# Three products summed by transfer, another order of casts, conversions and memory in a tuned attention and two-network kernel

## The chip, the cores and the metric

One core of one Trainium2 chip runs the whole program. The metric is the device time of one execution in microseconds; for the kernel before it is 1594.09 us, the median of three runs (1589.73 to 1597.51).

## The reference

```python
def _attn_ref(q, k, v, g_norm):                     # 8 batches, 8 heads, 576 tokens, head 64
    kv = np.einsum('bhsd,bhse->bhde', k, v)
    out = np.einsum('bhsd,bhde->bhse', q, kv)
    rms = np.sqrt(np.mean(out * out, axis=-1, keepdims=True) + 1e-06)
    return (out / rms * g_norm).astype(np.float32)
...
# x: [4608 tokens, 512]; each network has w_in [512, 2048] and w_out [2048, 512]
def _moe_ref(x, w_in, w_out):
    r = np.maximum(x @ w_in, 0.0)
    return (r * r @ w_out).astype(np.float32)
...
def _moe2_ref(x, w_in, w_out):
    h = x @ w_in
    return ((h * np.cos(h)) @ w_out).astype(np.float32)
```

The result is `_moe2_ref(_moe_ref(attention))`. Everything is in float32; the weights arrive as 64-bit floats.

## The kernel before

A matrix value is split into two parts, `h` (rounded by a cast on ScalarE) and `l` (the rest, subtracted on VectorE), and each product is three matmuls: h by h, h by l and l by h. The work has two stages.

Stage one (`run_chunks`, until about 500 us) computes attention and, for the first half of the first network's 2048 inner columns, both matrix products directly. Its sums leave PSUM in `evict` (L397) through the tile `ev` and are stored in the DRAM tensors `p_d`. Between its matmuls it converts the 64-bit weights (`conv_steps`, L165).

Stage two is the slot loop (`run_slots`, L825). A slot is (m, t, q): network m, token tile t, and a group q of 512 inner columns. The first network has two groups left per tile, the second four, and there are five tiles: 10 and 20 slots, k = 0 to 29. Three tiles are twice 512 tokens wide, two are twice 384 (`TILES`). In a slot each of the two matrix products is done as seven products of half-size blocks, numbered 0 to 6 and taken in the order 0, 1, 3, 2, 5, 4, 6. The first matrix product makes h from x blocks (`x_block`, L455: differences of four quarter blocks, cast and rest) and weights `wi`; the second makes output sums from blocks of y (`s_block`, L586: the differences t1, t2 and two more, then cast `gh` and rest `gl`) and weights `ws`. Between them stands the activation: relu and square, or five steps for h·cos(h) (`cos_1` to `cos_5`). The second product of slot k runs 1.25 slots after the first (`LAG2`), so TensorE alternates between the first product of one slot and the second product of an earlier one.

PSUM holds two pairs of banks, FA and FB for first products, SA and SB for second ones. Products 0, 3, 5, 6 add up in one pair, 1, 2, 4 in the other, so each product in a pair must be read before the next one adds to it. In nearly all slots product 1 starts from a copy of product 0, made by ScalarE from one bank to the other (`seed` for F, L650 for S); `HOLD` delays product 1 by a quarter of its length for that copy.

`drain_product` (L646) reads a finished second product and adds it to one of four sums in SBUF; `SUM_OF` names the sum: product 1 goes to (0,0), 2 and 5 to (1,1), 3 and 4 to (0,1), 6 to (1,0). In the first group of a tile in the second network ScalarE writes the first of them as a plain copy. Otherwise either VectorE adds from PSUM (L662), or, for the products in `BY_DMA` and not in the last slot, ScalarE copies PSUM to a tile `part` (L659, pool `t` with two buffers) and GpSimd issues a transfer that adds `part` to the sum:

```python
if m and i in BY_DMA and k < len(slots) - 1:
    part = blocks_of(t, temp([P, 2, 512], F32, "part"))
    nc.scalar.copy(out=part, in_=ps)
    nc.gpsimd.dma_start(out=e, in_=part, accum_op=ALU.add)
else:
    nc.vector.tensor_tensor(out=e, in0=ps, in1=e, op=ALU.add)
```

The order is written as a list of jobs, each with a place in slots (`at`, `pos`, L680); PH is the seventh of a slot that one product takes. The framework then orders each engine's instructions ahead of time and every engine runs its list in order, waiting where an input is not there or a buffer is not free. Seven conversions of the second network's weights run in the slot loop (`late_stream`, L730), each in steps (`Stream.place`, L697).

Memory: stage two's pools `c` (18 tiles: x, h, y, t and g blocks) and `t` (`part` and the temporaries of conversions) and the late conversions' raw tile lie where stage one's pools were (L880-882, opened from the right end of SBUF), so their first use waits until stage one has finished with what lies there.

Of the kernel before, what the change touches and what calls it, by code (L numbers as in the profile page):

```python
# [8 lines left out]
F32 = mybir.dt.float32  # L9
# [13 lines left out]
def kernel(  # L23
# [15 lines left out]
    nc = tc.nc  # L39
# [384 lines left out]
    ORDER = (0, 1, 3, 2, 5, 4, 6)  # L424
    W_OF = (0, 1, 3, 4, 6, 5, 2)
    BLOCKS = {(0, 0): 2, (1, 1): 5, (0, 1): 6, (1, 0): 7}
    S_ORDER = (0, 1, 3, 2, 5, 4, 6)
    BY_DMA = (4, 5, 1, 6)
    SEEDED = 2

    def seeded(k):
# [3 lines left out]
        return seeded(k) and k < len(slots) - 1  # L435

    HOLD = 9
    xb, wi, ws, kept, hs, ys, sums, quads = {}, {}, {}, {}, {}, {}, {}, {}

    def big(pool, dtype, name, ht):  # L440
# [81 lines left out]
    def t_tile(k, dtype, name):  # L522
        return big("c", dtype, name, TILES[slots[k][1]][1])
# [55 lines left out]
    def load_sum(k, d, j):  # L579
# [3 lines left out]
        for b, s0, done, size in pieces(t0 + j * ht, ht, TOK):  # L583
            nc.sync.dma_start(out=e[:, :, done:done + size], in_=p_d[b][:, 2 * d:2 * d + 2, s0:s0 + size])

    def s_block(k, i):  # L586
        m, t, q = slots[k]
        b11, b12, b21, b22 = (ys.get((k, b)) for b in ((0, 0), (0, 1), (1, 0), (1, 1)))

        def minus(out, x, y):  # L590
            nc.vector.tensor_tensor(out=out, in0=x, in1=y, op=ALU.subtract)
            return out

        if i == 3:
            ys[k, "t1"] = minus(t_tile(k, F32, "t"), b12, b11)
            ys[k, "t2"] = minus(t_tile(k, F32, "t"), b22, ys[k, "t1"])
        src = {
            0: lambda: b11,
            1: lambda: b21,
            2: lambda: ys[k, "t1"],  # L600
            3: lambda: ys[k, "t2"],
            4: lambda: b22,
            5: lambda: minus(b12, b22, b12),
            6: lambda: minus(b21, b21, ys[k, "t2"]),
        }[i]()
        gs[k, i] = h, l = [t_tile(k, F32R, f"g{n}") for n in "hl"]
        nc.scalar.copy(out=h, in_=src)  # L607
        nc.vector.tensor_tensor(out=l, in0=src, in1=as32(h), op=ALU.subtract)  # L608
# [77 lines left out]
    class Stream:  # L686
# [9 lines left out]

        def place(self, positions, after, skip=()):  # L697
            for k, (n, item) in enumerate(zip(positions, self.items)):
                steps = (0, 0.07, 0.15, 0.22, 0.3, 0.4, 0.62)
                if n < nA0:  # L700
                    steps = (0, 0.25, 0.5, 0.75, 1.0, 1.25, 1.4)
                if self.use != conv_w or item[0] == "one":
                    at(n, self.use, *item)
                    steps = (after,)
                for d in steps[:-1]:
                    at(n + d, conv_part, *item)
                if k not in skip:
                    at(n + steps[-1], self.advance)
# [20 lines left out]
    w_stream.place(w_at, 0.5, range(2 * NH - NRAW, 2 * NH - NRAW + 2))  # L729
    late_stream = Stream(load_w, conv_w, [("pairs", 1, p, 0) for p in range(1, 2 * NP)])  # L730
    at(pos(0.15), late_stream.advance)
    late_stream.place([pos(0.45 + 1.05 * k) for k in range(5)] + [pos(9.9), pos(10.85)], 0)

    kv_stream = Stream(load_kv, kv_mm, [(b, c) for b in range(B) for c in range(NSC)])
    starts = [(-13, 1), (-3, 0.8)] + [(-3 + 7 * (b - 1), 7 / (2 * NKC)) for b in range(2, B)]
# [24 lines left out]
    for k, (m, t, q) in enumerate(slots):  # L760
        if q == 0:
            for a in range(2):
                at(pos(k + (a - 6.8) * PH) if k else nA0 - 9, load_quads, m, t, a)
            for f, i in enumerate(ORDER):
                at(pos(k + X_AT[f] * PH) if k or f > 3 else nA0 - 7 + 1.5 * f, x_block, k, i)
        for f, i in enumerate(ORDER):
            at(pos(k + (f - 2.7) * PH) if k or f > 2 else nA0 - 5 + f / 2, load_wi, k, i)
        for f, i in enumerate(S_ORDER):
            at(pos(k + LAG2 + (f - 2.7) * PH), load_ws, k, i)
            at(pos(k + LAG2 + (f - (1.1 if f == 1 else 1.6)) * PH), s_block, k, i)  # L770
        if not seeded(k):
            at(pos(k + 1 * PH), keep, k, "m1", 0)
            at(pos(k + 2 * PH), add, k, (0, 0), 1, "m1")
        else:
            at(pos(k + 1 * PH), seed, k)
            at(pos(k + 2 * PH), whole, k, (0, 0), 1)
        at(pos(k + 3 * PH), keep, k, "u2", 3)
        at(pos(k + 4 * PH), keep, k, "m5", 2)
        at(pos(k + 5 * PH), add, k, (1, 1), 5, "m5")
        at(pos(k + 6 * PH), add, k, (0, 1), 4, "u2")  # L780
        at(pos(k + 7 * PH), whole, k, (1, 0), 6)
        chain = (cos_1, cos_2, cos_3, cos_4, cos_5) if m else (relu_1, relu_2)
        for b, f in BLOCKS.items():
            for a, fn in enumerate(chain):
                at(pos(k + (f + 0.25 * (a + 1)) * PH), fn, k, b)
        if m == 0 and q == 0:
            for n, dj in enumerate(((0, 0), (1, 1), (0, 1), (1, 0))):
                at(pos(k + LAG2 + (n - 2) * PH), load_sum, k, *dj)
# [36 lines left out]
    def run_slots():  # L825
# [10 lines left out]
        ]  # L836
        firsts = [(k, i) for k in range(len(slots)) for i in ORDER]
        steps1 = (x for k, i in firsts for x in first_product(k, i))
        todo = [(k, i) for k in range(len(slots)) for i in S_ORDER]
        steps2 = (x for k, i in todo for x in second_product(k, i))  # L840
        nf, ns = 12 * len(firsts), 0
        due = []
# [32 lines left out]
    with ExitStack() as early:  # L875
# [3 lines left out]

        right("pad", 1).tile([P, 56], F32, name="pad")  # L880
        pools["raw"] = right("conv", 2)
        x_p, g_p, ev_p, pools["t"] = (right(n, b) for n, b in (("x", XB), ("g", 3), ("ev", 2), ("tmp", 8)))
        with tc.tile_pool(name="att", bufs=1, side="right") as att_p:
            kvx = [att_p.tile([P, NKC, P], F32, tag=f"kvx{b}", name=f"kvx{b}") for b in range(2)]
            for x in kvx:
# [62 lines left out]
```

## Time and profile before

| | |
|---|---|
| profiled execution, device time | 1593.9 us |
| its span | 1592.1 us |
| TensorE busy (matmul) | 1542.6 us, 97% |
| VectorE busy | 1254.8 us, 79% |
| ScalarE busy | 1107.7 us, 70% |
| GpSimd busy | 105.5 us, 7% |
| mean granted clock of TensorE | 0.997 |
| transfers sum<-part | 43 of 512 KB, 24 of 384 KB |

The span runs from the first to the last instruction; the device time is a little longer. The shares are means over stages with different limits: which engine or wait decides is read stretch by stretch. In the rows the engines are PE (matmul) and PEld (weight load) for TensorE, DVE for VectorE, ACT for ScalarE, POOL for GpSimd and SP for the queue that issues most transfers; L and a number is a line of the kernel; `out<-in` names the tiles. Matmuls are pipelined, so a busy PE is not PE at its peak, but an idle one is lost time where PE sets the pace.

### The profile page before, as it was taken

Reading aid. Unit: us, or ns where it says so; the run is one execution under the profiler, and the core shown is the slowest. Engines: PE = TensorE matmul, PEld = TensorE weight load, DVE = VectorE, ACT = ScalarE, POOL = GpSimd, SP = SyncE. Lnnn points to the kernel's source line nnn. Section 1 sums busy time; section 2 is a strip of 40 time slices with the busy share of each in tenths; the row PEclk is TensorE's granted clock in tenths of the full one; section 3 lists DMA queues with packets and bytes.
Section 4 is the critical chain, followed back from the end, with each engine's and each line's share of the span. In section 5 each row is a group of like instructions: output and inputs, shape, how many; then the busy total and the mean of one; then the engine's idle time right before and its main releaser. Section 6 shows DMA issues by size and latency. Waiting matters only on the chain.

```text
span 1592.1 us, 24817 instructions
## 1 busy us (share of the span) xinstructions
PE 1542.6 (97%) x9104; PEld 1349.8 (85%) x9104; DVE 1254.8 (79%) x1676; ACT 1107.7 (70%) x1568; POOL 105.5 (7%) x117
## 2 busy tenths in 40 slices
PE   5999999999999999999999999999999999999997
PEld 4777777778887777888998899999998999999997
DVE  7988788788885898987879868766876687687576
ACT  6977677775444666665656778877887777778774
POOL 1100101111000000000000000000000001011010
PEclk9999999999999999999999999999999999999999
DMA  9758889866678989998999779987998799999994
GB/s 325 269 168 230 261 259 284 238 204 208 195 230 298 309 283 338 319 385 263 336 355 341 279 229 269 280 266 227 268 271 263 227 262 297 333 302 275 323 296 116
DMA packets 229160, 433.13 MB, mean 272 GB/s; under 512 B 18608, under 2 KB 144816, under 8 KB 229040
## 3 DMA queue, kind: packets, MB, share of 16 engines
q1 hardware_dynamic: 218624, 397.21, 74.2%
q0 software_dynamic: 10416, 34.35, 10.7%
q8 instruction: 72, 1.18, 0.3%
q14 instruction: 48, 0.39, 0.1%
HBM read 317.72 MB, written 81.79 MB: 251 GB/s over the span
## 4 chain that ended last, share of the span: by engine, by line
PE 77%; DMA 8%; DVE 6%; issue 4%; ACT 4%; SPq 0%; DVEq 0%; ACTq 0%; POOLq 0%
PE SB L631 14%; PE SA L631 14%; PE FB L508 13%; PE FA L508 13%; PE acc L416 10%; PE l L379 9%; DMA sum<-part 2%; PE o L379 1%; DMA ws_d<-raw 1%; PE ss L379 1%; DVE gl L608 1%; DMA xraw<-x_d 1%; DMA q<-in_qT 1%; DMA p_d<-ev 1%; DMA raw<-in_wA 1%
## 5 line engine op out<-in xcount | busy, mean ns | idle before, releaser
L508 PE MATMUL FA<-xh,wi 128*128 128x512 f32 (+1 forms) x840 | 300.0, 371 | 8.0 <-ACT h L545 3.3
L508 PE MATMUL FB<-xh,wi 128*128 128x512 f32 (+1 forms) x840 | 299.3, 370 | 0.0
L631 PE MATMUL SA<-ws,gh 128*128 128x256 f32 x1008 | 230.3, 282 | 5.5 <-ACT gh L607 5.5
L631 PE MATMUL SB<-ws,gh 128*128 128x256 f32 x1008 | 229.3, 282 | 2.0 <-ACT SB L650 1.9
L631 PEld LDWEIGHTS SA<-ws,gh 128*128 128x128 f32 x1008 | 181.9, 190 | 17.3 <-ACT gh L607 6.2
L631 PEld LDWEIGHTS SB<-ws,gh 128*128 128x128 f32 x1008 | 181.0, 189 | 14.0 <-ACT SB L650 3.3
L508 PEld LDWEIGHTS FA<-xh,wi 128*128 128x128 f32 x840 | 157.3, 188 | 20.5 <-ACT h L545 3.9
L575 DVE SCALAR_TENSOR_TENSOR y<-y,h 128x1024 f32<-128x1024 f32 (+1 forms) x80 | 89.3, 1116 | 108.4 <-ACT y L571 108.1
L508 PEld LDWEIGHTS FB<-xh,wi 128*128 128x128 f32 x840 | 157.3, 188 | 11.1
L631 PE MATMUL SB<-ws,gl 128*128 128x256 f32 x504 | 142.4, 282 | 1.5 <-DVE gl L608 1.5
L631 PE MATMUL SA<-ws,gl 128*128 128x256 f32 x504 | 142.4, 282 | 0.6 <-DVE gl L608 0.6
L608 DVE TENSOR_TENSOR gl<-y,gh 128x1024 fp32r<-128x1024 f32 (+1 forms) x100 | 111.2, 1113 | 34.7 <-ACT gh L607 33.5
L660 POOL DMA_DIRECT2D sum<-part x67 | 57.0, 851 | 1101.9 <-DMA wi<-wi_d 535.2
L557 ACT ACTIVATE y<-h,zerob 128x1024 int32<-128x1024 f32 (+1 forms) x80 | 85.3, 1066 | 40.7 <-DVE h L533 40.6
L416 PE MATMUL acc<-gh,wh 128*128 128x512 f32 x288 | 113.6, 395 | 0.0
L416 PE MATMUL acc<-gl,wh 128*128 128x512 f32 x288 | 112.8, 392 | 0.0
L416 PE MATMUL acc<-gh,wl 128*128 128x512 f32 x288 | 112.6, 391 | 0.0
L508 PE MATMUL FA<-xl,wi 128*128 128x512 f32 (+1 forms) x300 | 111.3, 371 | 0.0
L508 PE MATMUL FB<-xl,wi 128*128 128x512 f32 (+1 forms) x300 | 110.9, 370 | 0.0
L607 ACT CAST gh<-y 128x1024 fp32r<-128x1024 f32 (+1 forms) x100 | 95.0, 962 | 12.6 <-DVE y L575 7.4
L631 PE MATMUL SB<-gh,ws 128*128 128x512 f32 (+1 forms) x280 | 100.0, 370 | 2.9 <-ACT SB L650 1.1
L631 PEld LDWEIGHTS SB<-ws,gl 128*128 128x128 f32 x504 | 95.5, 190 | 7.8 <-DVE gl L608 2.4
(172 smaller groups left out, 3775.4 us busy)
## 6 DMA issues: line engine op xcount, KB each, us to landing
wi<-wi_d SPq DMA_DIRECT2D x210, 512.0 KB, 6.8
ws<-ws_d SPq DMA_DIRECT2D x210, 512.0 KB, 6.0
sum<-part POOLq DMA_DIRECT2D x43, 512.0 KB, 8.1
kvld<-in_kv SPq DMA_DIRECT2D x32, 512.0 KB, 6.7
ws_d<-raw SPq DMA_DIRECT2D x24, 448.0 KB, 4.1
q<-in_qT SPq DMA_DIRECT2D x32, 288.0 KB, 4.0
p_d<-ev SPq DMA_DIRECT2D x18, 512.0 KB, 3.8
sum<-part POOLq DMA_DIRECT2D x24, 384.0 KB, 7.9
```

What stands on the lines that cost most here:

```text
L379: nc.tensor.matmul(ps, a[:, 0, cs], m[:], start=(c == 0 and k == 0), stop=(c == NKC - 1 and k == 2))
L416: nc.tensor.matmul(o, a[:, cs], m[:], start=(f == 0 and n == 0), stop=(f == NH - 1 and n == 2), skip_group_check=True)
L508: nc.tensor.matmul(ps[:, pp, :], a, b, start=(n == 0 and (i in (0, 2) or i == 1 and not seeded(k))), stop=(n == 5), skip_group_check=True,)
L557: nc.scalar.activation(out=y.bitcast(I32), in_=hs[k, b], func=AF.Identity, bias=zerob)
L575: nc.vector.scalar_tensor_tensor(out=y, in0=y, scalar=-2.0 * math.pi, in1=hs.pop((k, b)), op0=ALU.add, op1=ALU.mult)
L607: nc.scalar.copy(out=h, in_=src)
L608: nc.vector.tensor_tensor(out=l, in0=src, in1=as32(h), op=ALU.subtract)
L631: nc.tensor.matmul(ps[:, b, :], lhs, rhs, start=(n == 0 and (m == 0 or b % 2 == 0) and (i in (0, 2) or i == 1 and not seeded_s(k))), stop= ...
L660: nc.gpsimd.dma_start(out=e, in_=part, accum_op=ALU.add)
```

## The change

`BY_DMA` becomes (1, 2, 4): in the second network, except in the first group's plain copies and in the last slot, products 1, 2 and 4 are added by transfer and 3, 5, 6 by VectorE. The order of second products is the usual one but for the last slot, where it is 0, 2, 3, 4, 5, 1, 6. The differences t1 and t2 become a job of their own (`s_sums`), at 0.35 product lengths after the start of product 0 (in the last slot 0.7 before it), and the block of product 3 moves from 0.4 to 1.1 product lengths after that start. In the first slot the three x blocks that are placed inside the loop (5, 4, 6) come one product length later. The late conversions move from 0.45, 1.5, 2.55, 3.6, 4.65, 9.9, 10.85 to 0.4, 2.45, 3.07, 4.45, 5.07, 10.5, 11.1 (in slots), and the steps of each are packed closer (the last at 0.45 instead of 0.62 slots). Of stage one's pools `ev` is opened first instead of third, so it lies nearer the right end, where stage two has its last pools.

```diff
--- before.py
+++ after.py
@@ -424,8 +424,7 @@
     ORDER = (0, 1, 3, 2, 5, 4, 6)
     W_OF = (0, 1, 3, 4, 6, 5, 2)
     BLOCKS = {(0, 0): 2, (1, 1): 5, (0, 1): 6, (1, 0): 7}
-    S_ORDER = (0, 1, 3, 2, 5, 4, 6)
-    BY_DMA = (4, 5, 1, 6)
+    BY_DMA = (1, 2, 4)
     SEEDED = 2
 
     def seeded(k):
@@ -435,6 +434,10 @@
         return seeded(k) and k < len(slots) - 1
 
     HOLD = 9
+
+    def s_order(k):
+        return ORDER if k < len(slots) - 1 else (0, 2, 3, 4, 5, 1, 6)
+
     xb, wi, ws, kept, hs, ys, sums, quads = {}, {}, {}, {}, {}, {}, {}, {}
 
     def big(pool, dtype, name, ht):
@@ -583,17 +586,16 @@
         for b, s0, done, size in pieces(t0 + j * ht, ht, TOK):
             nc.sync.dma_start(out=e[:, :, done:done + size], in_=p_d[b][:, 2 * d:2 * d + 2, s0:s0 + size])
 
+    def minus(out, x, y):
+        nc.vector.tensor_tensor(out=out, in0=x, in1=y, op=ALU.subtract)
+        return out
+
+    def s_sums(k):
+        ys[k, "t1"] = minus(t_tile(k, F32, "t"), ys[k, (0, 1)], ys[k, (0, 0)])
+        ys[k, "t2"] = minus(t_tile(k, F32, "t"), ys[k, (1, 1)], ys[k, "t1"])
+
     def s_block(k, i):
-        m, t, q = slots[k]
         b11, b12, b21, b22 = (ys.get((k, b)) for b in ((0, 0), (0, 1), (1, 0), (1, 1)))
-
-        def minus(out, x, y):
-            nc.vector.tensor_tensor(out=out, in0=x, in1=y, op=ALU.subtract)
-            return out
-
-        if i == 3:
-            ys[k, "t1"] = minus(t_tile(k, F32, "t"), b12, b11)
-            ys[k, "t2"] = minus(t_tile(k, F32, "t"), b22, ys[k, "t1"])
         src = {
             0: lambda: b11,
             1: lambda: b21,
@@ -696,7 +698,7 @@
 
         def place(self, positions, after, skip=()):
             for k, (n, item) in enumerate(zip(positions, self.items)):
-                steps = (0, 0.07, 0.15, 0.22, 0.3, 0.4, 0.62)
+                steps = (0, 0.06, 0.12, 0.17, 0.23, 0.3, 0.45)
                 if n < nA0:
                     steps = (0, 0.25, 0.5, 0.75, 1.0, 1.25, 1.4)
                 if self.use != conv_w or item[0] == "one":
@@ -729,7 +731,7 @@
     w_stream.place(w_at, 0.5, range(2 * NH - NRAW, 2 * NH - NRAW + 2))
     late_stream = Stream(load_w, conv_w, [("pairs", 1, p, 0) for p in range(1, 2 * NP)])
     at(pos(0.15), late_stream.advance)
-    late_stream.place([pos(0.45 + 1.05 * k) for k in range(5)] + [pos(9.9), pos(10.85)], 0)
+    late_stream.place([pos(n) for n in (0.4, 2.45, 3.07, 4.45, 5.07, 10.5, 11.1)], 0)
 
     kv_stream = Stream(load_kv, kv_mm, [(b, c) for b in range(B) for c in range(NSC)])
     starts = [(-13, 1), (-3, 0.8)] + [(-3 + 7 * (b - 1), 7 / (2 * NKC)) for b in range(2, B)]
@@ -762,12 +764,14 @@
             for a in range(2):
                 at(pos(k + (a - 6.8) * PH) if k else nA0 - 9, load_quads, m, t, a)
             for f, i in enumerate(ORDER):
-                at(pos(k + X_AT[f] * PH) if k or f > 3 else nA0 - 7 + 1.5 * f, x_block, k, i)
+                at(pos(k + (X_AT[f] + (0 if k else 1)) * PH) if k or f > 3 else nA0 - 7 + 1.5 * f, x_block, k, i)
         for f, i in enumerate(ORDER):
             at(pos(k + (f - 2.7) * PH) if k or f > 2 else nA0 - 5 + f / 2, load_wi, k, i)
-        for f, i in enumerate(S_ORDER):
+        for f, i in enumerate(s_order(k)):
             at(pos(k + LAG2 + (f - 2.7) * PH), load_ws, k, i)
-            at(pos(k + LAG2 + (f - (1.1 if f == 1 else 1.6)) * PH), s_block, k, i)
+            at(pos(k + LAG2 + (f - (1.1 if f == i == 1 else 0.9 if f == 2 and i == 3 else 1.6)) * PH), s_block, k, i)
+            if f == 1:
+                at(pos(k + LAG2 + (0.35 if i == 1 else -0.7) * PH), s_sums, k)
         if not seeded(k):
             at(pos(k + 1 * PH), keep, k, "m1", 0)
             at(pos(k + 2 * PH), add, k, (0, 0), 1, "m1")
@@ -836,7 +840,7 @@
         ]
         firsts = [(k, i) for k in range(len(slots)) for i in ORDER]
         steps1 = (x for k, i in firsts for x in first_product(k, i))
-        todo = [(k, i) for k in range(len(slots)) for i in S_ORDER]
+        todo = [(k, i) for k in range(len(slots)) for i in s_order(k)]
         steps2 = (x for k, i in todo for x in second_product(k, i))
         nf, ns = 12 * len(firsts), 0
         due = []
@@ -879,7 +883,7 @@
 
         right("pad", 1).tile([P, 56], F32, name="pad")
         pools["raw"] = right("conv", 2)
-        x_p, g_p, ev_p, pools["t"] = (right(n, b) for n, b in (("x", XB), ("g", 3), ("ev", 2), ("tmp", 8)))
+        ev_p, x_p, g_p, pools["t"] = (right(n, b) for n, b in (("ev", 2), ("x", XB), ("g", 3), ("tmp", 8)))
         with tc.tile_pool(name="att", bufs=1, side="right") as att_p:
             kvx = [att_p.tile([P, NKC, P], F32, tag=f"kvx{b}", name=f"kvx{b}") for b in range(2)]
             for x in kvx:
```

## Rows read from the trace of the kernel before

**Rows 1.** Stretches: length, busy us of PE, PEld, DVE, ACT, POOL, clock, DMA, GB/s.

```profile
500.00:514.00 14.00, 10.78 (x47) 8.26 (x46) 10.57 (x14) 7.11 (x9) 0.00 (x0) 1.00 0.94 329
548.00:650.00 102.00, 97.29 (x424) 78.74 (x423) 96.32 (x97) 67.31 (x69) 0.00 (x0) 1.00 0.89 302
878.00:893.00 15.00, 13.17 (x75) 11.13 (x74) 12.76 (x16) 10.85 (x12) 0.00 (x0) 1.00 0.86 291
893.00:1206.00 313.00, 313.00 (x2004) 283.46 (x2003) 235.66 (x203) 244.22 (x249) 24.68 (x29) 1.00 0.88 261
1350.00:1362.00 12.00, 10.47 (x74) 10.15 (x73) 7.21 (x8) 7.17 (x10) 0.89 (x2) 1.00 1.03 266
1465.00:1485.00 20.00, 16.69 (x109) 16.37 (x108) 9.21 (x11) 12.06 (x17) 2.55 (x3) 0.94 0.95 275
1566.20:1574.00 7.80, 3.67 (x19) 3.27 (x18) 5.57 (x6) 3.86 (x6) 0.85 (x1) 0.82 0.42 81
1574.00:1592.10 18.10, 12.16 (x95) 11.59 (x94) 10.86 (x12) 2.78 (x4) 0.00 (x0) 0.97 0.25 87
```

**Rows 2.** Chain of waits before 1481: start us, us, what.

```profile
1466.23 10.20 DMA sum<-part
...
1476.50 0.80 ACT part L659
...
1480.78 0.72 ACT h L545
```

**Rows 3.** Timeline of ScalarE, 501-509: start, us, instruction, idle before <- what ended it.

```profile
501.27 1.05 ACT L402 COPY ev<-acc 128x512 f32<-128x512 f32 x2
...
508.41 1.05 ACT L481 CAST xh<-xraw 128x1024 fp32r<-128x1024 f32 x1 [6.09 <-DMA p_d<-ev]
```

**Rows 4.** Timeline of ScalarE, 1353-1360.

```profile
1353.82 1.02 ACT L659 COPY part<-SB 128x1024 f32<-128x1024 f32 x1 [2.59 <-DMA sum<-part]
...
1358.52 0.83 ACT L607 CAST gh<-t 128x768 fp32r<-128x768 f32 x1 [2.24 <-DVE t L591]
...
1359.26 0.79 ACT L650 COPY SB<-SA 128x768 f32<-128x768 f32 x1
```

**Rows 5.** Timeline of VectorE and TensorE: product 2 drained, product 6 begun.

```profile
947.21 1.23 DVE L662 TENSOR_TENSOR sum<-SA,sum 128x1024 f32<-128x1024 f32 x1 [0.59 <-PE SA L631]
...
958.21 0.28 PE L631 MATMUL SB<-ws,gh 128*128 128x256 f32 x1
...
1525.23 0.96 DVE L662 TENSOR_TENSOR sum<-SA,sum 128x768 f32<-128x768 f32 x1 [0.30 <-PE SA L631]
...
1533.48 0.28 PE L631 MATMUL SB<-ws,gh 128*128 128x256 f32 x1
```

**Rows 6.** Timeline of POOL at 1355.

```profile
1355.12 0.85 POOL L660 DMA_DIRECT2D sum<-part  x1 [5.09 <-ACT part L659]
```

**Rows 7.** DMA issues at 937, 1332, 1393, 1548, 1564-1567: count, KB, us to landing.

```profile
sum<-part POOLq DMA_DIRECT2D x1, 512.0 KB, 7.2
...
sum<-part POOLq DMA_DIRECT2D x1, 512.0 KB, 7.6
...
sum<-part POOLq DMA_DIRECT2D x1, 384.0 KB, 7.7
...
sum<-part POOLq DMA_DIRECT2D x1, 384.0 KB, 7.5
...
sum<-part POOLq DMA_DIRECT2D x2, 384.0 KB, 3.8
```

**Rows 8.** The tile `part`, 900 to 1345: its transfers.

```profile
DMA to landing us min/median/max: 6.3/8.3/11.7
```

**Rows 9.** Timeline of TensorE at 1362: product 3 begun.

```profile
1362.88 0.28 PE L631 MATMUL SA<-ws,gh 128*128 128x256 f32 x1
```

**Rows 10.** Timeline of VectorE in the last slot.

```profile
1562.38 0.96 DVE L575 SCALAR_TENSOR_TENSOR y<-y,h 128x768 f32<-128x768 f32 x1 [2.68 <-ACT y L571]
...
1587.65 0.96 DVE L662 TENSOR_TENSOR sum<-SB,sum 128x768 f32<-128x768 f32 x1 [1.20 <-PE SB L631]
```

## The prediction

> **What bounds the kernel now.** I read four views, in this order. First the table of stretches [rows 1]. Between 893 and 1206 us TensorE is busy 313.00 of 313 us: there the number and size of the matmuls set the time, and the change neither adds nor drops one. It can win only TensorE's idle time, which the other rows of the table locate. From 500 us on, where the slot loop begins, it is 14 - 10.78 = 3.22 us at the start of the loop, 102 - 97.29 = 4.71 from 548 to 650, 1.83 at the step to the second network (878-893), 1.53 at 1350-1362, 3.31 at 1465-1485, and in the last slot 4.13 (1566-1574) and 5.94 (after 1574). Two rows also show a granted clock under 1.00 where TensorE had stood idle for over 3 us, 0.94 and 0.82: part of each ran at the lower level, 1.2 GHz. That costs about 0.06 x 20 = 1.2 us and 0.18 x 7.8 = 1.4 us more.
>
> Next the chain of waits through 1481 us [rows 2]. A transfer sum<-part, issued at 1466.23, lands 10.20 us later. Only then can ScalarE write the next `part` (1476.50; there are two buffers), and what stands behind that copy in its queue is late, last `h` at 1480.78, for which TensorE waits. Then ScalarE's timeline at the start of the loop [rows 3]: the cast xh at 508.41 stood 6.09 us for a store of stage one's sums, since its tile lies on the memory that the store reads. Last, ScalarE around 1355 [rows 4]: `part` waits 2.59 us for a transfer, then the cast of a difference 2.24 us for VectorE, and the copy from SA to SB, which the next product needs, stands behind both.
>
> **The change part by part.** It is summed against the profiled execution's own 1593.9 us (span 1592.1), 0.2 us under the median of the runs shown.
>
> *Accumulating transfers.* With products 4, 5, 1, 6 there are 67; with 1, 2, 4 there are 31 of 512 KB and 17 of 384 KB, 48 in all. ScalarE loses 19 copies to `part`. VectorE gains 19 drains, 12 of 1.23 us and 7 of 0.96 us [rows 5], 21.5 us. From 893 to 1206 it is idle for 313 - 235.66 = 77 us [rows 1], a quarter of the time, which hides them; without that cover they cost at most those 21.5 us. No two of the three transfers belong to neighbouring products any more, so a `part` buffer is free in time: the wait of [rows 2] goes with its clock loss, 3.31 + 1.2 us.
>
> But a wait is added. Products 2 and 5 go into the same sum, (1,1). Until now VectorE added 2 and a transfer 5. Now 2 is the transfer, and VectorE's drain of 5, one product later, waits until it has landed. Product 6 writes the PSUM bank of 5, so TensorE's first matmul of 6 waits for that drain. So it is in the slots of the second network that add to earlier sums, but for the last: 9 of 512 columns and 5 of 384.
>
> The time there is: at 512 columns product 2 ends at 947.21 and 6 starts at 958.21, 11.0 us later; at 384 it is 1525.23 to 1533.48, 8.25 us [rows 5]. The time needed is a place in ScalarE's queue (0.6 us, part of one instruction ahead of it), the copy (1.02 us; 0.80 at 384 [rows 2, 4]), 0.28 us to the issue on POOL [rows 4, 6], the landing L, and the drain (1.23 or 0.96): L + 3.1 and L + 2.65 us. For L I take the transfers that run alone today, as 2 will: those of product 1. At 512 columns there are nine, the first 7.2 and the last 7.6 us; at 384 five, 7.7 and 7.5 [rows 7]. With 7.4 it just fits at 512 (10.5 of 11.0); I put 1 us for all nine slots. With 7.6 it doesn't at 384: 10.25 - 8.25 = 2.0 us in each of four slots, 8 us (the fifth stands in the tail below). The bounds: two transfers at the very end land in 3.8 us [rows 7], and then neither waits; the longest from 900 to 1345 takes 11.7, with a median of 8.3 [rows 8], and that would be 3.8 x 9 + 6.1 x 4 = 59 us. Behind the waiting drain VectorE holds a last step of y, the next gl and a cos step; by the order of the products TensorE needs that gl after product 6, so they cost nothing while the drain is done before 6 is due.
>
> The Trainium skill, "DMA: Bandwidth & Descriptors", section "Anatomy of one DMA — SWDGE (gpsimd) path", fits a transfer issued by GpSimd with 2.0 us plus its bytes over 436 GB/s: an estimate of 3.2 us for 512 KB. By that the drain of 5 would never wait, and the 9 us of this part would be 0. The rows show more than twice as much; only the one of 3.8 us is near it.
>
> *ScalarE's order.* t1 and t2 keep their place. The cast of t2 for product 3 moves from 0.4 to 1.1 of a product after the start of product 0, behind the copy SA to SB; the 1.53 us of [rows 1] at 1350-1362 go. Late is now gl of product 3: copy 0.79, cast 0.83 and a subtraction of 0.96 us follow each other, 2.6 us from the start of the copy, at 1359.26 [rows 4, 5], while product 3 begins at 1362.88 [rows 9], 3.6 us after it. 1 us is left; where VectorE's queue is full some of 29 slots will overrun it: 0.5 us in all, between 0 and 6.
>
> *Conversions, and the memory of stage one's sums.* Of seven conversions most move out of the x blocks' stretches, with their loads and stores on SP's queue, whose weights are read slots later. From 548 to 650 VectorE is busy for 96.32 of 102 us [rows 1], so work taken from the crowded places is worth something: 3.2 of the 4.71 us and 1.2 of the 1.83 (bounds: nothing, since the same work comes back elsewhere, and all). At the loop's start the cast no longer stands for the store and its block comes a product later; a conversion stood ahead of the copies of the last sums as well (they start at 501.27) [rows 3]. But by the pools' sizes the temporaries of the first conversion now lie on those sums, so it waits for the store, with whatever stands behind it on VectorE and ScalarE. I take 2.0 of the 3.22 us; between a loss of 3 us (one more wait like 6.09 less half) and a gain of 3.2.
>
> *The last slot.* Product 1, whose block leaves the cosine chain last, goes from second to sixth place, its load of ws with it, so TensorE need not idle at 1566-1570. Then VectorE is the limit: from 1562.38 [rows 10] it has two last steps and one middle step of y, 4 differences, 7 gl, 7 drains and now the previous slot's drain of 6, 22 instructions. The 12 after 1574 took 10.86 us, 0.905 each [rows 1]: 19.9 us. With a wait of 2 us for the previous slot's transfer, as above, it is done near 1584.3 rather than 1587.65 + 0.96 = 1588.6 [rows 10], 4.3 us, of which I take 3.5. Without that wait it is 6.3; if VectorE stays as loosely filled as now, 0.
>
> *The sum.* Gains: 4.5 + 1.5 + 3.2 + 1.2 + 2.0 + 3.5 = 15.9. Losses: 8 + 1 + 0.5 = 9.5. 1593.9 - 15.9 + 9.5 = 1587.5 us.
>
> **The rivals.** *No wait for the transfer* (L up to 5.6 us at 384 columns): the transfers are fewer and apart, and what slows them may be their own company. Against it: the lone ones of today already take 7.2 us and more. The 9 us come back and 1 us in the tail: 1577.5.
>
> *The new wait grows* (the other side). If L is that of transfers with company, product 6 stalls in nearly every one of these slots: 4 x (L - 5.6) + 9 x (L - 7.9). From L = 8.4 us on this eats all gains; at 9.5 it is 15.6 + 14.4 = 30 us, and the time 1593.9 - 15.9 + 0.5 + 30 = 1608.5. For it speaks the median of 8.3; against it that product 4 ends two products after 2, when the transfer of 2 has landed.
>
> *Idle time only moves.* VectorE is as full as before, so the conversions and the late gl stall TensorE elsewhere: the 6.4 us of the early stretches come back, and the time is 1594.
>
> **How the numbers follow.** Forecast 0.40, no wait 0.27, idle time moves 0.19, wait grows 0.14. The forecast's own range is 1582 to 1594. A measurement of this kernel tells about 0.5%, 8 us, from no change, so "faster" is below 1586.1 and "slower" above 1602. Faster: nearly all of no wait and four tenths of the forecast, 0.42. Slower: most of the grown wait and a little of the moved idle time, 0.16. Same: 0.42. The range for 8 in 10 goes from a little under the no-wait case, 1575, into the grown wait, 1604.
>
> **What would show it.** 48 transfers sum<-part; no `part` on ScalarE that waits for one; 14 drains on VectorE whose idle time ends with sum<-part, each followed by a gap of TensorE before product 6, about 2 us at 384 columns and none at 512; no clock under 1.00 near 1481; xh not waiting for p_d; in the last slot product 1 sixth and VectorE without gaps. If TensorE shows no gap before product 6, the first rival holds; if gaps of over 1 us stand at 512 columns too, the second. The prediction is wrong if new gaps stand at places named nowhere here.

## The result and the profile after

The changed kernel takes 1606.68 us, the median of four runs (1604.48 to 1609.93); the kernel before takes 1592.57 us beside it (four runs, 1589.73 to 1597.51). The ratio is 1.0082, with a 95% interval from 1.0062 to 1.0103: slower by 13 us (10 to 16), where 6.6 us faster was forecast. The profiled execution took 1604.48 us (span 1602.7 us, mean granted clock 0.993), so it was the fastest of the four: its span is 10.6 us longer than that of the kernel before, a little less than the medians' difference.

The stretches of [rows 1] in the changed kernel, and the one from 514 to 530 beside them (length, busy us of PE, PEld, DVE, ACT, POOL, granted clock, DMA share, GB/s); the last goes to its own end:

```profile
500.00:514.00 14.00, 13.17 (x59) 10.62 (x58) 4.18 (x4) 6.25 (x7) 0.00 (x0) 1.00 0.96 323
514.00:530.00 16.00, 8.43 (x26) 6.38 (x25) 12.17 (x14) 7.48 (x8) 0.00 (x0) 0.68 0.85 304
548.00:650.00 102.00, 98.40 (x432) 80.56 (x431) 92.76 (x89) 63.41 (x65) 0.00 (x0) 1.00 0.86 295
878.00:893.00 15.00, 15.00 (x84) 13.39 (x83) 13.81 (x14) 9.45 (x10) 0.00 (x0) 1.00 0.98 364
893.00:1206.00 313.00, 306.66 (x1947) 276.90 (x1946) 244.12 (x214) 236.09 (x240) 17.00 (x20) 0.99 0.82 252
1350.00:1362.00 12.00, 10.79 (x79) 10.52 (x77) 5.25 (x6) 9.11 (x11) 0.85 (x1) 1.00 1.04 355
1465.00:1485.00 20.00, 20.00 (x145) 19.98 (x144) 13.97 (x16) 15.13 (x21) 1.70 (x2) 1.00 0.87 243
1566.20:1574.00 7.80, 7.80 (x58) 7.80 (x57) 5.52 (x6) 4.08 (x6) 0.85 (x1) 1.00 0.92 281
1574.00:1602.70 28.70, 22.23 (x174) 21.25 (x172) 22.36 (x26) 11.63 (x15) 0.84 (x1) 0.96 0.31 85
```

These rows show the same times as [rows 1], but not the same work: around 1480 us the changed kernel is about 15 us behind. Each trace holds 9104 matmuls, in the same order but for the last slot and some neighbours that change places. So it can be read off at which matmul, counted from the start, the changed kernel falls behind or catches up, and by how much; the times are those of the kernel before. It gains 2.7 us from 500 to 514, loses 10.5 from 514 to 530, gains 1.8 from 530 to 650, loses 3.6 from 878 to 910 and 7.5 from 910 to 1566, and gains 5.6 us from there to the end.

So the gaps that the change aimed at are gone, but new ones stand close to them and elsewhere. The last slot's gain stays. At 500-514 TensorE is idle for 0.83 us instead of 3.22; right behind, from 514 to 530, it is idle for 7.57 us, where it had no idle time, at a granted clock of 0.68. The row 878-893 shows none, but from 896 to 907 there are 4.1 of the 6.34 us that TensorE is idle from 893 to 1206. And the row 1465-1485 shows none, but a wider one, first of the kernel before and then of the changed kernel, does:

```profile
1465.00:1500.00 35.00, 31.69 (x215) 31.37 (x214) 20.32 (x23) 24.14 (x33) 2.55 (x3) 0.95 0.96 318
1465.00:1500.00 35.00, 33.11 (x223) 32.72 (x223) 25.01 (x29) 24.41 (x32) 2.55 (x3) 0.95 0.94 293
```

The old gap, in which ScalarE waited for a `part` buffer, and its clock loss are gone, 4.9 us. But 10 us of work ahead of its place stands a new gap of 1.89 us with a clock loss of its own, which together cost 3.6 us. Three kinds of gaps make up the loss.

*TensorE waits for VectorE, which waits for a transfer.* From the list of waits (us in total, times, longest us), the drains on VectorE and the transfers' median time to landing:

```profile
DVE sum L664 <- DMA sum<-part: 31.1, 11, 4.5
...
sum<-part POOLq DMA_DIRECT2D x31, 512.0 KB, 7.3
```

In the kernel before no drain on VectorE waited for a transfer. The drain at 1423.40 below is a twelfth, which the profile puts down to TensorE. The timeline of a slot of 384 columns, changed kernel (start us, us, engine, instruction, idle before <- releaser):

```profile
1416.53 0.84 POOL L662 DMA_DIRECT2D sum<-part  x1 [8.12 <-ACT part L661]
...
1423.40 0.96 DVE L664 TENSOR_TENSOR sum<-SB,sum 128x768 f32<-128x768 f32 x1 [3.68 <-PE SA L633]
...
1424.46 0.36 PE L633 MATMUL SB<-ws,gh 128*128 128x256 f32 x1 [1.14 <-ACT part L661]
```

Product 2's transfer is issued at 1416.53 and lands at 1423.31, 6.78 us later. The drain of product 5 starts at 1423.40 and ends at 1424.36, and product 6, which overwrites that bank, starts at 1424.46. The profile names other releasers in both brackets (a wait for several semaphores is put down to one of them), but the times fit the transfer and the drain alone. There are six such gaps, 7.5 us in all: one of 1.8 us in a slot of 512 columns (at 1362.45) and five of 0.5 to 2.0 us in the slots of 384 (here and below a gap is the time from the matmul before to this one, less the usual distance of the two, which is up to 0.2 us more than the bracket).

The second form reaches TensorE on a detour. Timeline of a slot of 512 columns, same kernel:

```profile
965.09 1.23 DVE L664 TENSOR_TENSOR sum<-SB,sum 128x1024 f32<-128x1024 f32 x1 [3.20 <-DMA sum<-part]
966.23 1.22 DVE L578 SCALAR_TENSOR_TENSOR y<-y,h 128x1024 f32<-128x1024 f32 x1
967.37 1.22 DVE L610 TENSOR_TENSOR gl<-y,gh 128x1024 fp32r<-128x1024 f32 x1
968.50 1.22 DVE L564 SCALAR_TENSOR_TENSOR y<-y,h 128x1024 f32<-128x1024 int32 x1
969.75 1.06 ACT L570 ACTIVATE y<-y 128x1024 f32<-128x1024 f32 x1 [1.55 <-DVE y L564]
970.72 1.00 ACT L543 COPY FA<-FB 128x1024 f32<-128x1024 f32 x1
...
971.77 0.50 PE L511 MATMUL FA<-xh,wi 128*128 128x512 f32 x1 [0.96 <-ACT FA L543]
```

Product 6 is not late here. But VectorE has stood still for 3.20 us, and the cosine step L564 behind the drain starts at 968.50. ScalarE needs its result for the step L570, and behind that step, in ScalarE's queue, is the copy from FB to FA with which product 1 of the next first product begins. TensorE waits for the copy. Six gaps before a product 1 of a first product, and one before the copy from SA to SB (1559.65), stand from 971 to 1560 and sum to 5.7 us. The chain is shown here for one of them; that the wait is behind all seven rests on a run below, in which the wait and all seven gaps are gone.

*The first conversion on the moved memory.* Timeline at 507-523, same kernel:

```profile
507.02 0.81 SPq L145 DMA_DIRECT2D raw<-in_wB  x2
...
514.13 0.70 DVE L111 TENSOR_SCALAR e<-raw 128x1024 uint32<-128x1024 uint32 x1 [4.13 <-DMA raw<-in_wB]
...
519.12 0.83 ACT L192 CAST wh<-raw 128x768 fp32r<-128x768 f32 x1 [3.11 <-DVE raw L125]
...
520.71 1.04 ACT L192 CAST wh<-raw 128x1024 fp32r<-128x1024 f32 x1 [0.76 <-DVE raw L175]
...
521.66 1.02 ACT L530 ACTIVATE m<-FB 128x1024 f32<-128x1024 f32 x1
...
522.73 0.80 PE L511 MATMUL FB<-xh,wi 128*128 128x512 f32 x1 [7.57 <-ACT m L530]
```

The conversion's raw tile now lies on the sums' tiles, so its load is issued only when their last store has landed (507.00). In the kernel before it was issued at 493.40, and the first step ran at 499.48:

```profile
493.40 0.81 SPq L145 DMA_DIRECT2D raw<-in_wB  x2
...
499.48 0.69 DVE L111 TENSOR_SCALAR e<-raw 128x1024 uint32<-128x1024 uint32 x1 [3.42 <-PE acc L416]
```

Now the load lands at 513.94, all steps follow one another behind it, and both casts of the conversion stand in ScalarE's queue ahead of the copy `m` that empties FB. TensorE waits 7.57 us, and part of the stretch behind the gap runs at the lower clock level (1.2 GHz).

*Two conversions too close to each other.* Timeline at 599-612, same kernel:

```profile
599.74 1.51 SPq L145 DMA_DIRECT2D raw<-in_wB  x2
...
608.48 0.69 DVE L111 TENSOR_SCALAR e<-raw 128x1024 uint32<-128x1024 uint32 x1 [6.21 <-DMA raw<-in_wB]
...
609.20 1.15 ACT L112 ACTIVATE e<-e,expb 128x1024 int32<-128x1024 int32 x1 [3.66 <-DVE e L111]
...
610.26 1.01 ACT L543 COPY FA<-FB 128x1024 f32<-128x1024 f32 x1
...
612.14 0.47 PE L633 MATMUL SA<-gh,ws 128*128 128x512 f32 x1 [2.08 <-ACT FA L543]
```

There is one raw buffer. The load for the conversion at 3.07 is issued when the last store of the one at 2.45 has landed (599.72), so its first instruction on VectorE waits 6.21 us, and the copy FB to FA is late behind L112. Near 896 a cast of the last conversion, at 11.1, stands on ScalarE ahead of `gh` (gaps of 2.3 and 1.1 us).

### The profile page after: what moved, and what is told of

It reads as the page before. It is cut to its first block, busy times and chain, and to the rows that moved or that the text cites. A ratio compares the mean times of both kernels' runs of the same rounds, so it can differ in the third digit from the quotient of the medians.

```text
span 1602.7 us, 24720 instructions
## 1 busy us (share of the span) xinstructions
PE 1546.4 (96%) x9104; PEld 1352.9 (84%) x9104; DVE 1274.6 (80%) x1695; ACT 1094.8 (68%) x1549; POOL 89.4 (6%) x98
## 4 chain that ended last, share of the span: by engine, by line
PE 44%; issue 31%; DVE 10%; DMA 8%; ACT 4%; POOL 1%; SPq 1%; POOLq 0%; DVEq 0%; ACTq 0%
PE acc L416 9%; PE l L379 7%; PE SB L633 6%; PE FA L511 6%; PE FB L511 6%; PE SA L633 6%; DVE gl L610 2%; DMA sum<-part 1%; DMA ws_d<-raw 1%; DMA raw<-in_wB 1%; DMA ws<-ws_d 1%; POOL sum L662 1%; PE o L379 1%; DVE sum L664 1%; PE ss L379 1%
## 5 line engine op out<-in xcount | busy, mean ns | idle before, releaser
L664 DVE TENSOR_TENSOR sum<-SB,sum 128x1024 f32<-128x1024 f32 (+1 forms) x62 | 69.0, 1113 | 57.5 <-PE SB L633 27.3
L570 ACT ACTIVATE y<-y 128x1024 f32<-128x1024 f32 (+1 forms) x80 | 77.9, 973 | 52.7 <-DVE y L564 52.5
L662 POOL DMA_DIRECT2D sum<-part x48 | 40.8, 849 | 1132.1 <-ACT part L661 565.9
```

The lines of the kernel that those rows point to most:

```text
L570: nc.scalar.activation(out=y, in_=y, func=AF.Sin, scale=math.pi)
```

## The experiments

Ratios are to the kernel before on the same chip, with 95% intervals; one per mille is 1.6 us.

**Which part costs the time?** Four kernels undo or do one part alone. Their expectations are written for a chip on which the kernel before takes 1592.6 us; here it took 1597.3. By their ratios the four come to 1603.2, 1591.5, 1595.1 and 1600.2 us on that scale.

```diff
-        ev_p, x_p, g_p, pools["t"] = (right(n, b) for n, b in (("ev", 2), ("x", XB), ...))
+        x_p, g_p, ev_p, pools["t"] = (right(n, b) for n, b in (("x", XB), ("g", 3), ("ev", 2), ...))
```

> The changed kernel with only the order of stage one's pools as before (ev third). Theory 'memory': the load of the first late conversion's raw weights no longer waits for the store of stage one's sums, so the conversion is not late, its casts do not stand ahead of ScalarE's copy m, and the stretch 515-528 us loses its 7.7 us of idle time and the 2.6 us of half clock: about 1596 us. Theory 'transfers' (VectorE's drain of product 5 waits for the transfer of 2, and that is where the time went): no more than 2 us back, 1604 to 1607 us.

Measured: 1607.63 us, 1.0067 (1.0049 to 1.0085). The order of the pools gives back 2.4 us of 13, and the intervals of the two kernels overlap. The gap near 522 is gone all the same:

```profile
514.00:530.00 16.00, 16.00 (x71) 13.04 (x70) 7.11 (x7) 13.39 (x15) 0.00 (x0) 1.00 1.02 339
```

So the memory is the cause of that gap, but not of the loss.

```diff
-    BY_DMA = (1, 2, 4)
+    BY_DMA = (4, 5, 1, 6)
```

> The changed kernel with only products 4, 5, 1, 6 by transfer, as before. Theory 'memory': the 10 us at 515-528 stay, and the gaps before product 6 (7.5 us) go while the wait of part near 1481 us may come back (4.5 us): 1602 to 1605 us. Theory 'transfers': all that was lost comes back, 1593 us or less.

Measured: 1595.11 us, 0.9993 (0.9981 to 1.0004). With the old transfers the whole loss is gone, 14.2 us, though the gap near 522 is still there:

```profile
514.00:530.00 16.00, 8.39 (x26) 6.40 (x25) 11.06 (x14) 7.00 (x7) 0.00 (x0) 0.68 0.86 305
```

The kernel before with the pools' new order alone (the reverse of the first edit):

> The kernel before with only ev opened first. Theory 'memory': the first conversion's load waits for the store here too; its casts come late: between 4 and 10 us slower, 1597 to 1602 us, with a gap of TensorE behind ScalarE's copy m and a granted clock under 1 near 525 us. Theory 'transfers': no change, 1591 to 1594 us, or 1 to 2 us faster, since the cast xh no longer waits for the store.

Measured: 1599.72 us, 1.0016 (1.0006 to 1.0027): 2.5 us, as much as undoing it gives and less than the 4 to 10 us of theory 'memory'. TensorE's gap behind a conversion is there too, here at 521.69 us:

```profile
521.69 0.79 PE L508 MATMUL FB<-xh,wi 128*128 128x512 f32 x1 [5.16 <-ACT m L527]
```

The kernel before with `BY_DMA = (1, 2, 4)` alone:

> The kernel before with only products 1, 2, 4 by transfer. As forecast before the result: the wait near 1481 us goes (4.5 us), gaps of TensorE before product 6 come (about 2 us in each of four slots of 384 columns), and seeds of F wait behind VectorE in some slots (4 us): 1594 to 1601 us. Theory 'transfers': 1603 us or more, about all of the loss. If the added wait costs nothing: 1588 us.

Measured: 1603.38 us, 1.0048 (1.003 to 1.0066): 7.7 us. On the scale of the expectation that is in the first range (1594 to 1601) and under that of 'transfers': alone, the transfers cost, by the middle of the interval, over half of the loss and not nearly all. (The 4 us for the seeds of F in that expectation weren't in the prediction; they come from the trace after.) Its list of waits has the new one, in the size of the changed kernel:

```profile
DVE sum L662 <- DMA sum<-part: 33.1, 12, 4.7
```

**Is it the wait, or VectorE's 19 additional drains?** The changed kernel with one more product taken from the transfers and given to VectorE:

```diff
-    BY_DMA = (1, 2, 4)
+    BY_DMA = (1, 4)
```

> The changed kernel with transfers for products 1 and 4 alone: product 2 is added by VectorE, like products 3, 5 and 6. VectorE then has 14 more additions than in the changed kernel and 33 more than in the kernel before (0.95 to 1.22 us each), and no addition is left that follows a transfer into the same sum within the next product. Times for a chip on which the kernel before takes 1597 us. Theory 'wait': the loss is VectorE standing still for the transfer of product 2 (31.1 us in 11 places in the changed kernel's trace), so it goes with the wait although VectorE works more: 1594 to 1600 us, and no addition that waits for a transfer. Rival 'load': the loss is the 19 additions (21 us of VectorE) that the change put on VectorE, which make the y chain and the freeing of the banks late; then 14 more make it worse: 1612 to 1620 us. The forecast's own mechanism (only the stall of product 6 counts, about 7.5 us in the trace after) gives 1602 to 1604 us.

Measured: 1589.96 us, 0.9964 (0.9951 to 0.9976): 19 us under the changed kernel, 6 under the kernel before. VectorE works more and nothing waits for a transfer. The stretch 950 to 1560 in three kernels (columns as above): before, changed, and this one.

```profile
950.00:1560.00 610.00, 604.54 (x4027) 568.64 (x4027) 451.75 (x430) 471.58 (x531) 51.01 (x60) 1.00 0.91 276
```

```profile
950.00:1560.00 610.00, 599.25 (x3967) 561.47 (x3967) 464.11 (x440) 453.02 (x505) 35.61 (x42) 1.00 0.85 260
```

```profile
950.00:1560.00 610.00, 610.00 (x4080) 575.11 (x4079) 489.92 (x467) 454.85 (x506) 25.44 (x30) 1.00 0.81 255
```

VectorE is busy for 489.92 us instead of 464.11, and TensorE has no idle time left. Both forms of the gap, before product 6 and before the copy FB to FA, are gone. So the rival 'load' falls, and so does the forecast's own accounting, which expected only the 7.5 us before product 6 to come back. The time is even under the range of theory 'wait'. This kernel also has 14 copies to `part` on ScalarE and 14 transfers fewer than the changed one, which could be another cause; but the changed kernel with the old transfers has 19 of each more, and there the loss went as well. What both lack is the wait of VectorE, so that wait is the loss of the transfers.

**The last slot alone.** The kernel before with

```diff
+    def s_order(k):
+        return ORDER if k < len(slots) - 1 else (0, 2, 3, 4, 5, 1, 6)
```

and t1, t2 formed apart from block 3, with their old places in all other slots.

> The kernel before with one thing changed: the last slot's second products in the order 0, 2, 3, 4, 5, 1, 6 with the sums t1 and t2 formed later there. On a chip where the kernel before takes 1597 us. Forecast's term: 3.5 us less, 1592 to 1595 us. Rival 'the order gives nothing': TensorE stands still elsewhere in the last slot, 1596 to 1598 us. The trace of the changed kernel with its transfers undone, where the excess of the last 50 us is 2.8 us against 9 in the kernel before, speaks for 5 to 6 us: 1590 to 1592 us.

Measured: 1591.61 us, 0.9968 (0.9954 to 0.9981): 5.1 us less (3.0 to 7.3).

**The conversions.** The changed kernel with the old places and steps:

```diff
-    late_stream.place([pos(n) for n in (0.4, 2.45, 3.07, 4.45, 5.07, 10.5, 11.1)], 0)
+    late_stream.place([pos(0.45 + 1.05 * k) for k in range(5)] + [pos(9.9), pos(10.85)], 0)
```

> The changed kernel with the late conversions at the places and steps of the kernel before. On a chip where the kernel before takes 1597 and the changed kernel 1610 us. Theory 'spacing': the new places took away 7 us of stalls near 554, 564, 573, 622, 649, 881 and 891 us, but brought 8.8 us near 612, 621, 628 and 897 to 907 us (one raw buffer, two conversions 0.62 slots apart), so undoing them gives 0 to 3 us back: 1607 to 1610 us; the 7.6 us near 522 stays, since that comes from the memory. Rival, the forecast's term (the places are worth 4.4 us): 1613 to 1615 us.

Measured: 1607.28 us, 1.0065 (1.0048 to 1.0083), 2.7 us under the changed kernel; the intervals overlap. From 500 to 950 TensorE is busy for 438.67 us instead of 433.67 in the changed kernel and 440.24 in the kernel before. That the new places gain 4.4 us is excluded, since they would then have to be missed here. The gap near 522 did not stay as it was: it is 5.46 us here and 5.16 with the pools alone, both with the conversions at the old places, so 2 us of its 7.57 come with the new places and steps.

**Do the gains stand without the wait?** The changed kernel with the old transfers, the old pools and three of the conversions at their old places:

> The changed kernel with the transfers of the kernel before (products 4, 5, 1 and 6) and the memory pools in the old order, and the first and the two last of the late conversions at their old places; what stays of the change is the order of the second products (ScalarE's too), the sums t1 and t2 by themselves, and conversions two to five. On a chip where the kernel before takes 1597 us and the changed kernel with the transfers alone undone 1595. If the stalls add: 7.8 us near 522 with 2 us of half clock, and 3 us near 897, come off: 1581 to 1586 us. Rival 'what one stall gives the next takes': 1590 to 1596 us.

Measured: 1591.41 us, 0.9968 (0.9956 to 0.9979). The gap near 522 is gone, but there are 2.9 us at 609 (0.8 with the transfers alone undone) and 1.6 and 1.4 at 506 and 513 (one of 1.0): the time is in the range of the rival, that one stall gives what the next takes.

The changed kernel with `BY_DMA = (1, 4)` and the first late conversion at 1.0 instead of 0.4 (the last two at 9.9 and 10.85):

> The changed kernel with transfers for products 1 and 4 alone, and three of the late conversions elsewhere: the first at 1.0 slots in place of 0.4, the two last at 9.9 and 10.85 as in the kernel before. On a chip where the kernel before takes 1597 us and the changed kernel with products 1 and 4 alone 1591. If the stall near 522 (7.2 us and 2 us of half clock) came from the raw tile that lies on the moved memory, it goes once the conversion starts later, and some 2 us near 895 to 907 go as well: 1579 to 1584 us. Rival 'moves on': the conversion at 1.0 holds TensorE up at its new place as those at 0.45 and 1.5 did in the kernel before: 1587 to 1591 us.

Measured: 1583.4 us, 0.992 (0.99 to 0.9941): 7 us under the same kernel without the new places, and at the upper end of the first theory's range.

The same move of the first conversion alone, in the changed kernel:

> The changed kernel with the first late conversion at 1.0 slots in place of 0.4, nothing else. On a chip where the kernel before takes 1597 us and the changed kernel 1610. If the stall near 522 (7.6 us, and 2.6 us of half clock behind it) is that of a conversion whose raw tile can't be loaded until the stores from the moved memory have landed at 507 us, it goes: 1599 to 1603 us. Rival 'the memory is worth 2.5 us', as undoing the order of the pools and moving them alone have shown: the stall comes back elsewhere, 1606 to 1609 us.

Measured: 1605.71 us, 1.0054 (1.0035 to 1.0074), 4.5 us under the changed kernel with overlapping intervals, between the two theories. The gap is 2.3 us instead of 7.6:

```profile
514.00:530.00 16.00, 13.87 (x54) 11.01 (x53) 9.72 (x12) 9.49 (x10) 0.00 (x0) 0.89 0.84 280
```

**The order alone**, the kernel before with block 3 and t1, t2 of every slot at the new places and the products in the old order:

> The kernel before with block 3 of every slot formed earlier, the sums t1 and t2 apart from it, and so ScalarE's and VectorE's order changed near the products 1 and 3; the order of the products stays, in the last slot too. On a chip where the kernel before takes 1597 us. Forecast's term: 1.5 us less between 1350 and 1362: 1595 to 1596 us. Rival 'nothing': the stall near 1361 is that of ScalarE's copy from one bank to the other in any order: 1597 us.

Measured: 1594.11 us, 0.999 (0.9976 to 1.0003): 1.6 us, as forecast, but not told from nothing. Its row at 1465-1485 is worth a look:

```profile
1465.00:1485.00 20.00, 17.98 (x124) 17.34 (x124) 10.08 (x12) 13.93 (x19) 2.56 (x3) 1.00 0.96 272
```

The order alone shortens the idle time of [rows 1] there from 3.31 to 2.02 us and avoids the loss of clock, with 67 transfers still there (one execution).

**Do the parts add up?** 7.7 - 1.6 - 5.1 us for transfers, order and last slot is 1.0. The changed kernel with pools, conversions and x blocks as before:

> The changed kernel with the pools, the conversions and the x blocks of the first slot as in the kernel before: what stays is the transfers of products 1, 2 and 4, the order in all slots and the last slot's order. On a chip where the kernel before takes 1597 us. The single parts measured so far are +7.7 us for the transfers in the kernel before, -1.6 for the order, -5.1 for the last slot. Theory 'they add': 1597 - 5.1 - 1.6 + 7.7 = 1598 us. Rival 'the transfers cost more beside the order', as undoing them in the changed kernel gave back 14.2 us: the order alone already shortens the stall near 1482 that the transfers would take away, 1597 - 6.7 + 14.2 = 1604.5 us, and then the rest of the change (pools, conversions, x blocks) costs 5 to 6 us.

Measured: 1603.58 us, 1.0049 (1.0034 to 1.0065), 7.8 us and not 1. Transfers and order aim at the same gap near 1482, and beside the order the transfers have less to win; together they still bring the whole wait (38.3 us in 12 places in this kernel). In their company the transfers cost 7.8 + 1.6 + 5.1 = 14.5 us, as undoing them had shown, and the pools, conversions and x blocks cost the remaining 13.1 - 7.8 = 5.3 us.

The traces say the same part by part. The table gives, matmul by matmul as above, how many us later (or, with a minus, earlier) than the kernel before each kernel gets through three stretches of work; it is one execution of each, and up to 500 us they differ by -1.0 to 1.8 us.

| kernel | 500 to 910 | 910 to 1566 | last slot |
|---|---|---|---|
| changed | 9.8 | 7.5 | -5.6 |
| changed, old transfers | 9.0 | -3.0 | -5.8 |
| changed, transfers 1 and 4 | 8.0 | -8.3 | -5.2 |
| changed, old pools | 4.1 | 15.7 | -5.5 |
| changed, old conversions | 3.3 | 9.8 | -5.2 |
| pools alone | 4.4 | -0.2 | 0.7 |
| transfers alone | 1.5 | 7.7 | -0.3 |
| order, last slot, transfers 1, 2, 4 | 0.6 | 12.0 | -4.4 |
| order, last slot, transfers 1 and 4 (below) | -0.7 | -8.2 | -5.3 |

The middle column goes by the transfers first of all: whatever else is changed, it is a loss with products 1, 2, 4 and a gain with 1 and 4. The first column goes by pools and conversions: one of them alone goes with 3.3 to 4.4 us, both with 8 to 10. With products 1, 2, 4 the middle column is anything from 7.5 to 15.7 us, and the trace of the changed kernel, of its fastest run, has the smallest of these.

**Versions that beat both.** The kernel before with the last slot's order and `BY_DMA = (1, 4)`:

> The kernel before with two things changed: the last slot's second products in the order 0, 2, 3, 4, 5, 1, 6, and transfers for products 1 and 4 alone, so that VectorE makes 33 additions more and no addition follows a transfer into its sum within the next product. On a chip where the kernel before takes 1597 us, and the last slot's order alone gives 1592. Theory 'wait': the stall near 1482 (3.3 us and its loss of clock), in which ScalarE waits for a buffer of part, goes, and the 1.8 us near 1361 may: 1585 to 1589 us. Rival 'load': 33 additions more on VectorE delay the y chain: 1593 us or more.

Measured: 1582.79 us, 0.9915 (0.9894 to 0.9935). And with the new order in all slots as well:

> As the run of the order and the transfers of products 1, 2 and 4, but with transfers for products 1 and 4 alone, so that no addition waits for a transfer. On a chip where the kernel before takes 1597 us and the kernel before with the last slot's order and transfers 1 and 4 takes 0.9915 of it, 1583.4. If TensorE has no idle time left from 950 to 1560 us in that kernel, the order in all slots can add nothing there: 1581 to 1585 us. If the order is worth its 1.6 us by itself: 1580 to 1582.

Measured: 1582.4 us, 0.9923 (0.991 to 0.9936), the same. Between this kernel and the one of 1603.58 us the only difference is product 2 by VectorE or by transfer: 0.0126, 20 us. The order is worth nothing that could be told from noise once the wait is gone. From the changed kernel with transfers 1 and 4 (0.9964) this one differs in pools, conversions and x blocks alone: these cost 6.5 us there, beside the 5.3 above.

## Why the prediction was wrong

Two terms failed, and the two errors are about equally large: the wait for the transfer of product 2, and the conversions with the memory.

*The step that failed: "so they cost nothing while the drain is done before 6 is due".* That sentence was about what stands behind the waiting drain on VectorE, and it looked at one consumer, the gl that product 6 doesn't need yet. The cosine step in the same queue has another: ScalarE, and behind that step the copy FB to FA, on which TensorE depends within 2 to 3 us. The stall on VectorE was counted only where product 6 was late. Those gaps were sized well in sum: 8 + 1 us forecast, 7.5 in the trace, though the 1.8 us in one slot of 512 columns, whose transfer landed after 8.8 us, is the prediction's own sign for the rival "The new wait grows". The landing times were also right (6.1 to 8.8 us for the waiting slots of 512 KB and 6.4 to 8.1 for those of 384 KB, 4.4 for the last, where 7.4 and 7.6 were taken), and there were 48 transfers, 12 of the 14 drains named show the wait, and no `part` waits for a transfer. What was left out are the seven indirect gaps, 5.7 us in the trace, and the lost clock behind the gap at 1487, 0.05 x 35 = 1.7 us from 1465 to 1500. Direct gaps, indirect gaps and clock make 7.5 + 5.7 + 1.7 = 14.9 of the 15.8 us between the changed kernel's trace and the one with transfers 1 and 4 from 910 to 1566; by the medians of two pairs of kernels the wait costs 19 to 20 us, where 9 were forecast.

*The transfers as a whole.* Forecast: 4.5 us gained near 1481, 9 lost, so 4.5 lost. Measured: 7.7 lost alone, 14.5 in the company of the other parts. The gain near 1481 did come, but the order of ScalarE takes part of it anyway, and the sum treated the two as independent. The rival "The new wait grows" gave 1608.5 us and was on the right side, though by another mechanism: it needed landings of 9.5 us, and those stayed at 7.3.

*That VectorE's idle time hides 21.5 us of additional drains* was right, and more so than used: with 33 more drains instead of 19 TensorE has no idle time from 950 to 1560. The quarter of idle time hid that work, but not the waiting: 31.1 us of it on VectorE, in a queue that runs in order, moved everything behind it.

*Conversions and memory.* Forecast 3.2 + 1.2 + 2.0 = 6.4 us gained, measured 5.3 lost for these parts together. The gaps at 550-570 and the cast that waited for the store went as forecast; those at 881-891 went too, but others of 4.1 us came right behind them, at 896-907. For the first conversion the prediction put its temporaries on the sums' memory and bounded the wait for the store by 3 us, "one more wait like 6.09 less half"; it is 7.57 us and its clock, since it is the raw tile that lies there, and its load, five steps on VectorE and two casts follow one another after that store. That a conversion 0.62 slots after another waits for the only raw buffer was not looked at. The rival "Idle time only moves" had this mechanism, but took it for no loss. Measured alone, the pools cost 2.5 us, less than their gap of 5.16 us shows: the trace gives 2.8 us of it back at 500-514, where the cast no longer waits. Single executions of one kernel differ by up to 11 us (1599.09 to 1610.12 with the transfers alone), so a closer account can't be given.

*The last slot* was worth 5.1 instead of 3.5 us; 3.5 is inside the interval, but every trace with the new order there gains 4.4 to 5.8 us. And *ScalarE's order* came out as forecast, 1.6 for 1.5, by the middle of an interval that includes nothing; that agreement may be luck.

In sum: 1.6 and 5.1 us of gains against 14.5 and 5.3 us of losses is 13.1, the measured difference. That sum closes because 14.5 and 5.3 were taken as remainders; with the two costs measured by pairs of kernels, 14.2 and 6.5, it is 14.0 us, inside the measured 10 to 16.

## What to carry to other kernels

When an operation on a busy, ordered engine gets a wait, price the delay of everything that stands behind it and follow each of those to the tensor engine, through the other engines' queues too; that its own consumer is in time isn't enough. The accumulating transfers held nothing up here where nothing touched their target until they had landed: give them to products whose sum is next needed several products later (1 and 4 here), and let the engine with idle time do the pair that shares a sum in sequence. Gains that aim at the same gap are not to be added.

## What was not expected of the hardware

Fewer transfers into the sums landed barely sooner: the medians at 512 KB are 8.1 us with 67 of them, 7.3 with 48 and 7.4 with 34. The estimate of 3.2 us from the Trainium skill ("DMA: Bandwidth & Descriptors", section "Anatomy of one DMA — SWDGE (gpsimd) path") is met by none of these medians: accumulating transfers beside a DMA share of 0.81 to 0.91 take over twice as long. And a shorter gap cost TensorE its clock in one kernel while a longer one did not in another: from 1465 to 1500 the granted clock was 0.95 in the changed kernel with one gap of 1.89 us (1487.13), and 1.00 with one of 2.75 us (1491.80) in the same kernel with the first conversion at 1.0. Why isn't shown.
